# A linear attention and two expert MLPs: the W_out ring of eight swept forth and back, layer 2's conversion spread, g split half a step ahead

## The chip, the core and the metric

The kernel runs on one core of a Trainium2 chip. The metric is the device time of one execution in microseconds (us). TensorE (PE) multiplies, VectorE (DVE) and ScalarE (ACT) do the element-wise work, and SyncE (SP) issues nearly all DMAs, in the order in which they stand in its queue; GpSimd (POOL) does next to nothing.

## The reference

A linear attention with decay over 4 batches, 8 heads, 768 positions and head size 64 gives x of 3072 tokens by 512 features. Two MLPs follow it, each 512 to 2048 to 512:

```python
for t in range(S):
    state = gamma * state + einsum('bhd,bhe->bhde', k[:, :, t], v[:, :, t])
    y[:, :, t] = scale * einsum('bhd,bhde->bhe', q[:, :, t], state)
x = y as (3072, 512)
h = x @ w_in;   g = h * sigmoid(1.702 * h);                     x = g @ w_out      # layer 1
h = x @ w_in2;  g = max(h, 0) + alpha * min(h, 0);              x = g @ w_out2     # layer 2
```

The weights of the MLPs come as float64 and the output is float32.

## The kernel before, in words

**Precision.** Every operand of the MLPs is split into a high and a low half (fp32r); a product is hi·hi + hi·lo + lo·hi, three matmuls of 128x512. A weight slice (`in` or `out`, 16 of each per layer) comes as float64 words in a buffer `ld`; `conv_words`, `conv_f32`, `conv_hi` and `conv_lo` make the two halves on ACT and DVE, and for layer 2 `store` writes them to HBM at once (`wc` for W_in, `wo` for W_out). For W_in, `conv_sums` and `conv_split` add four sums of quarters per two slices (`shi`, `slo`, also stored into `wc`).

**Stages.** The first 250 us do the attention and the first two blocks of 512 tokens of layer 1. Then come five *pairs* of blocks, `PAIRS`: two of layer 1 and three of layer 2. A pair has 16 *half-steps*, numbered h = 0 to 79 over all pairs (`idx, q = divmod(h // 2, NQ)`): the even one is `quad_1`, 24 matmuls into PSUM tiles pa, px, pb, pd (L549), the odd one `quad_2`, 18 matmuls into pa, pb, pd. Seven products per two slices of W_in replace eight. Behind each product ACT or DVE adds (`u`, `u3`, `gw`, L571 to L604) and applies the activation, so that four tiles g come out of two half-steps. From half-step 9 on (`QLAG`), two *y-steps* follow each half-step: a y-step multiplies one tile g (128 features of the 2048, 512 tokens) with its slice of W_out, 12 matmuls into four tiles py (L473). 16 y-steps make a sweep, two sweeps (t = 0, 1) a pair. When the last half-step is done, 18 y-steps are left.

**g_split (L438, L439).** Before a y-step, ACT casts g to `gh` and DVE subtracts to get `gl`. `y_split` calls it for both y-steps of a half-step.

**Slots.** All these tiles but the W_in ring lie in 82 equal slots of 2 KB per partition. `take` pops the slot that has been free longest, `give` appends it. A tile that takes a slot must wait for the last reader of the tile before it: for `shi`, `slo`, `whi`, `wlo`, `wb` and `y` that is a DMA that stores them.

**Loads.** A pair's W_in comes as `g1` (1024 KB) and `g2` (768 KB) per two half-steps (`load_w`, L522 and L524), two ahead; each of the two buffers is free again when the product that reads it last is done. The slices of W_out come from HBM as `woh` and `wol` (256 KB each, `load_wo`, L543), one pair of tiles per y-step, four y-steps ahead (`WSTEPS`). The evacuated py goes out from `y` (L509) at the end of a sweep.

**Order.** A scheduler of the framework puts the instructions on the engines' queues; it follows priorities and its own idea of when each operand is ready. `W2_AT` is a table that says at which half-step each of the 32 conversions of layer 2 (m = 0 to 31) enters; m = 10 to 27 enter at half-steps 16 to 27.

Of the kernel before, what the change touches and what calls it, by code (L numbers as in the profile page):

```python
# [8 lines left out]
F32 = mybir.dt.float32  # L9
F32R = mybir.dt.float32r  # L10
# [13 lines left out]
NF = DFF // P  # L24
# [5 lines left out]
LEAD = 5  # L30
LAG = 1
QLAG = 9
WSTEPS = 4
WARM = 17
CS = 4
HP = 300
# [8 lines left out]
PAIRS = ((1, 1), (1, 2), (2, 0), (2, 1), (2, 2))  # L45
NQ = NF // 2
X_OF = ("b11", "t2", "t3", "t1", "b21", "t4", "b22")
ATT1 = 36
W2_AT = [7 + m // 2 for m in range(10)] + [16 + 2 * (m - 10) // 3 for m in range(10, 28)] + [34 + m - 28 for m in range(28, 32)]


@with_exitstack
def tile_linear_attention_two_mlps(ctx: ExitStack, tc, qk, kv, w1, w2, consts, alpha, out):
# [9 lines left out]
    nc = tc.nc  # L63
# [26 lines left out]
    wo = {  # L90
        (l, f): dram.tile([2, P, 512], F32, name=f"wo{l}_{f}", tag=f"wo{l}_{f}") for l in (1, 2) for f in range(NF)
    }
    stored = set()
# [4 lines left out]
    def take(name, shape=(P, 512), dtype=F32):  # L98
        i = free.popleft()
        t = spool.tile(list(shape), dtype, tag=f"s{i}", name=name)  # L100
        home[id(t)] = (i, t)
        return t

    def give(*ts):
        for t in ts:
            free.append(home.pop(id(t))[0])
# [329 lines left out]
    def g_split(g):  # L436
        gh, gl = take("gh", dtype=F32R), take("gl", dtype=F32R)
        nc.scalar.copy(out=gh, in_=g)  # L438
        nc.vector.tensor_tensor(out=gl, in0=g, in1=gh.bitcast(F32), op=ALU.subtract)  # L439
        give(g)  # L440
        return gh, gl
# [17 lines left out]
    def mlp_y(layer, j, ft, begin, end, carry, w):  # L459
        if begin:  # L460
            for e in range(NP):
                py[e] = ps_y.tile([P, BT], F32, tag=f"y{e}", name=f"py{e}")
        gh, gl = g_of.pop((layer, j, ft))
        wh, wl = w
        cols = lambda w, e: w[:, e * P:(e + 1) * P]
        prods = [(e, cols(w, e), gh) for e in range(NP) for w in (wh, wl)]
        prods += [(e, cols(wh, e), gl) for e in range(NP)]
        if carry == "last" or (end and carry == "first"):
            prods.sort(key=lambda p: p[0])
        seen = [0] * NP  # L470
        for e, w, g in prods:
            seen[e] += 1
            nc.tensor.matmul(  # L473
                out=py[e], lhsT=w, rhs=g, start=(begin and seen[e] == 1), stop=(end and seen[e] == 3)
            )
            if not end or seen[e] < 3:
                continue
            with tc.high_priority(HP):
                mlp_out(layer, j, e, carry)
        give(gh, gl)  # L480

    def mlp_out(layer, j, e, carry):
        y = take("y")
        if carry == "in":
            old = loaded["part", e // 2].rearrange("p (a b) -> p a b", a=2)[:, e % 2, :]
            nc.vector.tensor_tensor(out=y, in0=py[e], in1=old, op=ALU.add)
            if e % 2:
                done()
        elif carry == "last" and e == NP - 1:
            m = BT // 2  # L490
            nc.scalar.copy(out=y[:, :m], in_=py[e][:, :m])
            nc.vector.tensor_copy(out=y[:, m:], in_=py[e][:, m:])
            rows = slice(e * P, (e + 1) * P)
            nc.scalar.dma_start(out=out[rows, j * BT:j * BT + m], in_=y[:, :m])
            nc.sync.dma_start(out=out[rows, j * BT + m:(j + 1) * BT], in_=y[:, m:])
            return
        elif e % 2:
            nc.vector.tensor_copy(out=y, in_=py[e])
        else:
            nc.scalar.copy(out=y, in_=py[e])  # L500
        if carry == "out":
            dst = part[e // 2, :, e % 2, :]
        elif layer == 1:
            dst = xsd[2 + j // 2][e % 2, :, e // 2, j % 2, :]
            if e == NP - 1 and j % 2:
                stored.add(("x", 2 + j // 2))
        else:
            dst = out[e * P:(e + 1) * P, j * BT:(j + 1) * BT]
        (nc.scalar if carry == "last" and e % 2 else nc.sync).dma_start(out=dst, in_=y)  # L509
        give(y)  # L510
# [4 lines left out]
    def load_w(n):  # L515
        if n >= NQ * len(PAIRS):
            return
        layer, i = PAIRS[n // NQ][0], n % NQ
        need = [("in", layer, 2 * i), ("in", layer, 2 * i + 1), ("sums", layer, i)]
        assert all(k in stored for k in need), (n, need)  # L520
        g1 = xpool.tile([P, 4, 512], F32R, tag=f"xhi{(n + 1) % 2}", name="g1")
        nc.sync.dma_start(out=g1.bitcast(F32), in_=wc[layer, i][0:4].rearrange("g p c -> p g c"))  # L522
        g2 = xpool.tile([P, 4, 512], F32R, tag=f"xlo{(n + 1) % 2}", name="g2")
        nc.sync.dma_start(out=g2[:, 0:3].bitcast(F32), in_=wc[layer, i][4:7].rearrange("g p c -> p g c"))  # L524
        two = lambda t, u, n: tuple(t[:, m, 256 * n:256 * n + 256] for m in (u, u + 1))
        ring[n] = (
            two(g1, 0, 0), two(g1, 2, 1), two(g2, 0, 0), two(g1, 2, 0),
            two(g1, 0, 1), (g2[:, 2, 0:256], g2[:, 2, 256:512]), two(g2, 0, 1),
        )

    ysteps = [
        (idx, t, f) for idx in range(len(PAIRS)) for t in range(2) for f in range(NF)
    ]
    wring = {}

    def load_wo(n):
        if n >= len(ysteps):
            return
        layer, f = PAIRS[ysteps[n][0]][0], ysteps[n][2]
        assert ("out", layer, f) in stored  # L540
        wring[n] = take("woh", dtype=F32R), take("wol", dtype=F32R)
        for t, src in zip(wring[n], (0, 1)):
            nc.sync.dma_start(out=t.bitcast(F32), in_=wo[layer, f][src])  # L543

    def product(idx, q, n, ps, fresh):
        wh, wl = ring[idx * NQ + q][n]
# [63 lines left out]
    def y_split(n):  # L610
        idx, t, f = ysteps[n]
        with tc.high_priority(HG):
            g_of["y", t, f] = g_split(g_of.pop((idx, t, f)))

    def y_step(n):
        idx, t, f = ysteps[n]
        layer, pr = PAIRS[idx]
        carry = "last" if n == len(ysteps) - 1 else "first" if idx == len(PAIRS) - 1 else None
        g_of[layer, 2 * pr + t, f] = g_of.pop(("y", t, f))
        w = wring.pop(n)  # L620
        mlp_y(layer, 2 * pr + t, f, f == 0, f == NF - 1, carry, w)
        give(*w)
        load_wo(n + WSTEPS)


    per = BT // C
# [7 lines left out]
    def job(slot, fn, *args, load=()):  # L634
        jobs.setdefault(int(slot), []).append((fn, args, load))
# [8 lines left out]
    def convert(key, slot):  # L644
        job(slot, conv_words, key, load=(key,))
        job(slot + 1, conv_f32, key)
        job(slot + 2, conv_hi, key)
        job(slot + 2, conv_lo, key)
        if key[0] == "in" and key[2] % 2:
            i = key[2] // 2  # L650
            s = slot + 3 if key[1] == 2 else ATT1 + 1 + 4 * i if i < 4 else base + 2 * i - 6
            job(s, conv_sums, key[1], i)
            job(s + 1, conv_split, key[1], i)
# [11 lines left out]
    for ft in range(NF):  # L665
        pair = [("in", ft - ft % 2), ("in", ft - ft % 2 + 1), ("out", ft - ft % 2), ("out", ft - ft % 2 + 1)]
        for n, kind in enumerate(("in", "out")):
            m = 2 * ft + n
            lead = 2 * LEAD
            convert((kind, 1, ft), m - 2 * per + CS if ft < LEAD else lead + 1 + 1.1 * (m - lead))  # L670
            kind, f = pair[2 * (ft % 2) + n]
            convert((kind, 2, f), base + W2_AT[m])
            job(12 + m if ft < LEAD else ATT1 + 0.7 * (m - 10), store, (("in", "out")[n], 1, ft))
# [32 lines left out]
    def run(slot):  # L706
        todo = [(rank.index(fn) if fn in rank else len(rank), i) for i, (fn, _, _) in enumerate(jobs.get(slot, ()))]
        for _, i in sorted(todo):
            fn, args, _ = jobs[slot][i]
            fn(*args)  # L710
# [24 lines left out]
    def drop():  # L735
        for _ in range(len(waiting)):
            key = waiting.popleft()
            if key in stored:
                give(w_hi.pop(key), w_lo.pop(key))
            else:  # L740
                waiting.append(key)
# [17 lines left out]
        if s == NF + LEAD:  # L759
            load_w(0)  # L760
    load_w(1)
    for n in range(WSTEPS):
        load_wo(n)
    for s, step in queue:
        finish_step(s, step)
    drop()
    done_y = 0
    for h in range(2 * NQ * len(PAIRS)):
        idx, q = divmod(h // 2, NQ)
        if h >= QLAG:  # L770
            for n in range(2):
                y_split(done_y + n)
        (quad_2 if h % 2 else quad_1)(idx, q)
        run(base + h)
        drop()
        if h >= QLAG:
            for n in range(2):
                y_step(done_y)
                done_y += 1
    for n in range(done_y, len(ysteps)):  # L780
        y_split(n)
        y_step(n)


# [51 lines left out]
```

## Time and profile before

| | us |
|---|---|
| median of 3 runs | 1124.21 |
| lowest, highest | 1120.92, 1129.53 |
| the profiled execution | 1124.57 |
| its span | 1122.8 |

The profiled execution spends 1.8 us outside its span. PE is busy 1092.6 us (97%), DVE 678.2 (60%), ACT 548.2 (49%). TensorE's clock was granted in full but for one stretch in the middle. A DMA share of 1.0 means that all 16 DMA engines were busy all the time.

### The profile page before, as it was taken

Reading aid. Unit: us, or ns where it says so; the run is one execution under the profiler, and the core shown is the slowest. Engines: PE = TensorE matmul, PEld = TensorE weight load, DVE = VectorE, ACT = ScalarE, POOL = GpSimd, SP = SyncE. Lnnn points to the kernel's source line nnn. Section 1 sums busy time; section 2 is a strip of 40 time slices with the busy share of each in tenths; the row PEclk is TensorE's granted clock in tenths of the full one; section 3 lists DMA queues with packets and bytes.
Section 4 is the critical chain, followed back from the end, with each engine's and each line's share of the span. In section 5 each row is a group of like instructions: output and inputs, shape, how many; then the busy total and the mean of one; then the engine's idle time right before and its main releaser. Section 6 shows DMA issues by size and latency. Waiting matters only on the chain.

```text
span 1122.8 us, 15612 instructions
## 1 busy us (share of the span) xinstructions
PE 1092.6 (97%) x5633; PEld 897.8 (80%) x5633; DVE 678.2 (60%) x1162; ACT 548.2 (49%) x1081; POOL 0.2 (0%) x4
## 2 busy tenths in 40 slices
PE   8899999999999999997999999999999999999998
PEld 6688787888888877875887888888888888888887
DVE  6899855365688785756666555764454764353530
ACT  7787745254575554544545444453343553343520
POOL 0000000000000000000000000000000000000000
PEclk9999999999999999998999999999999999999999
DMA  8899979278999979979979879568647377556731
GB/s 294 270 302 289 302 271 311 84 266 308 334 305 372 361 264 376 353 252 384 346 258 348 313 272 313 160 232 282 188 158 255 130 238 251 183 206 220 218 129 37
DMA packets 146700, 292.88 MB, mean 261 GB/s; under 512 B 13120, under 2 KB 23744, under 8 KB 146624
## 3 DMA queue, kind: packets, MB, share of 16 engines
q1 hardware_dynamic: 146192, 291.43, 75.7%
q8 instruction: 44, 0.72, 0.3%
q10 hardware_dynamic: 432, 0.47, 0.1%
q14 instruction: 32, 0.26, 0.1%
HBM read 227.88 MB, written 63.96 MB: 260 GB/s over the span
## 4 chain that ended last, share of the span: by engine, by line
PE 81%; DMA 11%; ACT 3%; DVE 3%; SPq 2%; issue 1%; DVEq 0%; ACTq 0%
PE py L473 42%; PE pb L549 9%; PE pd L549 8%; PE pa L549 8%; PE ph L450 5%; PE px L549 4%; DMA ld<-w 4%; DMA wc<-shi 2%; PE px L314 1%; PE sc L281 1%; PE px L304 1%; DMA wc<-wb 1%; DMA wc<-slo 1%; DMA g<-wc 1%; DMA wol<-wo 1%
## 5 line engine op out<-in xcount | busy, mean ns | idle before, releaser
L473 PE MATMUL py<-gh,woh 128*128 128x512 f32 x640 | 243.4, 391 | 11.8 <-ACT gh L438 10.9
L473 PE MATMUL py<-gh,wol 128*128 128x512 f32 x640 | 243.0, 390 | 1.0 <-DMA wol<-wo 1.0
L473 PE MATMUL py<-gl,woh 128*128 128x512 f32 x640 | 172.0, 389 | 0.0
L439 DVE TENSOR_TENSOR gl<-gw,gh 128x512 fp32r<-128x512 f32 x160 | 108.1, 688 | 95.1 <-ACT gh L438 76.2
L438 ACT CAST gh<-gw 128x512 fp32r<-128x512 f32 x160 | 97.6, 617 | 135.1 <-PE py L473 91.5
L473 PEld LDWEIGHTS py<-gh,woh 128*128 128x128 f32 x640 | 120.6, 189 | 38.1 <-ACT gh L438 11.8
L473 PEld LDWEIGHTS py<-gh,wol 128*128 128x128 f32 x640 | 120.7, 189 | 26.4 <-DMA wol<-wo 1.4
L473 PEld LDWEIGHTS py<-gl,woh 128*128 128x128 f32 x640 | 120.1, 188 | 25.0
L431 DVE SCALAR_TENSOR_TENSOR gw<-t,nalpha,gw 128x512 f32<-128x512 f32 x96 | 72.0, 750 | 78.2 <-ACT gw L430 77.9
L429 ACT ACTIVATE t<-gw 128x512 f32<-128x512 f32 x72 | 45.2, 628 | 100.8 <-DVE gw L580 81.3
L549 PE MATMUL pb<-xohi,g 128*128 128x512 f32 x320 | 86.3, 390 | 2.8 <-DMA g<-wc 2.8
L549 PE MATMUL pa<-xohi,g 128*128 128x512 f32 x320 | 87.6, 393 | 0.2 <-DMA g<-wc 0.2
L549 PE MATMUL pd<-xohi,g 128*128 128x512 f32 x320 | 85.8, 389 | 0.0
L549 PEld LDWEIGHTS pb<-xohi,g 128*128 128x128 f32 x320 | 59.8, 188 | 16.4 <-DVE cvt L166 3.6
L549 PEld LDWEIGHTS pd<-xohi,g 128*128 128x128 f32 x320 | 60.0, 188 | 12.9 <-ACT xohi L388 0.4
L549 PEld LDWEIGHTS pa<-xohi,g 128*128 128x128 f32 x320 | 59.3, 188 | 13.6 <-DMA g<-wc 0.6
L274 ACT ACTIVATE v<-ld,cst 128x64 f32<-128x64 f32 x168 | 44.4, 336 | 33.1 <-DMA ld<-kv 32.8
L156 ACT ACTIVATE cvt<-ld 128x512 f32<-128x512 f32 x64 | 43.0, 671 | 32.2 <-DMA ld<-w 20.5
L574 DVE TENSOR_TENSOR u<-px,u 128x512 f32<-128x512 f32 x40 | 27.6, 689 | 45.8 <-PE px L549 41.0
L473 PE MATMUL py<-gh,whi 128*128 128x512 f32 x128 | 51.9, 406 | 2.1 <-ACT gh L438 2.1
L450 PE MATMUL ph<-xhi,whi 128*128 128x512 f32 x128 | 51.4, 401 | 1.6 <-ACT xhi L360 1.5
L473 PE MATMUL py<-gh,wlo 128*128 128x512 f32 x128 | 50.3, 393 | 0.0
(92 smaller groups left out, 1679.6 us busy)
## 6 DMA issues: line engine op xcount, KB each, us to landing
g<-wc SPq DMA_DIRECT2D x40, 1024.0 KB, 7.0
woh<-wo SPq DMA_DIRECT2D x160, 256.0 KB, 5.2
wol<-wo SPq DMA_DIRECT2D x160, 256.0 KB, 5.3
ld<-w SPq DMA_DIRECT2D x64, 512.0 KB, 5.4
g<-wc SPq DMA_DIRECT2D x40, 768.0 KB, 6.7
ld<-qk SPq DMA_DIRECT2D x21, 512.0 KB, 5.1
ld<-kv SPq DMA_DIRECT2D x21, 512.0 KB, 4.8
ld<-xsd SPq DMA_DIRECT2D x20, 512.0 KB, 6.4
```

Of the source, the lines that this page charges most:

```text
L156: nc.scalar.activation(out=t, in_=w1, func=AF.Abs, scale=2.0**-112)
L274: nc.scalar.activation(out=v[:, h, :], in_=vt[:, h * D:(h + 1) * D], func=AF.Copy, scale=decay_v[:, h:h + 1])
L281: nc.tensor.matmul(out=ps[s][:, p, :], lhsT=kt[r, p * C:(p + 1) * C], rhs=qt[r, p * C:(p + 1) * C], start=True, stop=True,)
L304: nc.tensor.matmul(out=px[:, p, :], lhsT=state[:, p, :], rhs=qt[:, p * C:(p + 1) * C], start=(p == 0), stop=False, skip_group_check=True,)
L429: nc.scalar.activation(out=t, in_=src, func=AF.Relu, scale=-1.0)
L431: nc.vector.scalar_tensor_tensor(out=g, in0=t, scalar=nalpha[:, ft:ft + 1], in1=g, op0=ALU.mult, op1=ALU.add)
L438: nc.scalar.copy(out=gh, in_=g)
L439: nc.vector.tensor_tensor(out=gl, in0=g, in1=gh.bitcast(F32), op=ALU.subtract)
L450: nc.tensor.matmul(out=ph, lhsT=w[:, k * P:(k + 1) * P], rhs=x[:, k, :], start=(n == 0), stop=(n == len(prods) - 1),)
L473: nc.tensor.matmul(out=py[e], lhsT=w, rhs=g, start=(begin and seen[e] == 1), stop=(end and seen[e] == 3))
L549: nc.tensor.matmul(out=ps, lhsT=w[:, k * P:(k + 1) * P], rhs=xo[idx, n, k][part_], start=(fresh and m == 0), stop=(m == len(prods) - 1), s ...
L574: nc.vector.tensor_tensor(out=u, in0=px, in1=u, op=ALU.add)
```

## The change

Three edits.

- `WSTEPS` goes from 4 to 8, and the second sweep of each pair runs through the slices backwards. The ring is now keyed by layer and slice: a slice that is used again within the next 16 y-steps stays, so that the eight slices of a turning point are loaded once for both sweeps. `load_wo` fills the ring up to eight slices as soon as places are free. 96 slices are loaded in all, where 160 were.
- In `W2_AT`, m = 10 to 21 enter at half-steps 16 to 27, one each, and m = 22 to 31 at half-steps 32 to 39, in the third pair.
- `y_split` for the y-steps of half-step h is emitted behind quad h - 1, ahead of the y-steps of h - 1; it was emitted ahead of quad h.

```diff
-WSTEPS = 4
+WSTEPS = 8
...
-W2_AT = [7 + m // 2 for m in range(10)] + [16 + 2 * (m - 10) // 3 for m in range(10, 28)] + [34 + m - 28 for m in range(28, 32)]
+W2_AT = [7 + m // 2 for m in range(10)] + [16 + m - 10 for m in range(10, 22)] + [32 + 4 * (m - 22) // 5 for m in range(22, 32)]
...
     ysteps = [
-        (idx, t, f) for idx in range(len(PAIRS)) for t in range(2) for f in range(NF)
+        (idx, t, f if t == 0 else NF - 1 - f) for idx in range(len(PAIRS)) for t in range(2) for f in range(NF)
     ]
+    wkey = [(PAIRS[idx][0], f) for idx, _, f in ysteps]
     wring = {}
 
     def load_wo(n):
-        if n >= len(ysteps):
-            return
-        layer, f = PAIRS[ysteps[n][0]][0], ysteps[n][2]
-        assert ("out", layer, f) in stored
-        wring[n] = take("woh", dtype=F32R), take("wol", dtype=F32R)
-        for t, src in zip(wring[n], (0, 1)):
-            nc.sync.dma_start(out=t.bitcast(F32), in_=wo[layer, f][src])
+        for key in wkey[n:n + 2 * WSTEPS]:
+            if key in wring:
+                continue
+            if len(wring) == WSTEPS or ("out",) + key not in stored:
+                return
+            wring[key] = take("woh", dtype=F32R), take("wol", dtype=F32R)
+            for t, src in zip(wring[key], (0, 1)):
+                nc.sync.dma_start(out=t.bitcast(F32), in_=wo[key][src])
...
-        w = wring.pop(n)
-        mlp_y(layer, 2 * pr + t, f, f == 0, f == NF - 1, carry, w)
-        give(*w)
-        load_wo(n + WSTEPS)
+        mlp_y(layer, 2 * pr + t, f, n % NF == 0, n % NF == NF - 1, carry, wring[wkey[n]])
+        if wkey[n] not in wkey[n + 1:n + 2 * WSTEPS]:
+            give(*wring.pop(wkey[n]))
+        load_wo(n + 1)
...
-    for n in range(WSTEPS):
-        load_wo(n)
+    load_wo(0)
...
-    done_y = 0
+    split = 0
     for h in range(2 * NQ * len(PAIRS)):
         idx, q = divmod(h // 2, NQ)
-        if h >= QLAG:
-            for n in range(2):
-                y_split(done_y + n)
         (quad_2 if h % 2 else quad_1)(idx, q)
         run(base + h)
         drop()
+        if h >= QLAG - 1:
+            for n in range(split, split + 2):
+                y_split(n)
+            split += 2
         if h >= QLAG:
-            for n in range(2):
-                y_step(done_y)
-                done_y += 1
-    for n in range(done_y, len(ysteps)):
-        y_split(n)
+            for n in range(split - 4, split - 2):
+                y_step(n)
+    for n in range(split - 2, len(ysteps)):
+        if n + 2 < len(ysteps):
+            y_split(n + 2)
         y_step(n)
```

**Place 1, PE, half-steps 24 to 26 (in the second pair).** Matmuls of a quad (L549 before, L551 now) and of a y-step (py). Before:

```order
L473 MATMUL py_4559<-gl,woh 128x512
L473 MATMUL py_4560<-gl,woh 128x512
L549 MATMUL pd<-xohi,g_4923 128x512 x4
L549 MATMUL pd<-xolo,g_4923 128x512 x2
L549 MATMUL pa<-xohi,g_5131 128x512 x4
L549 MATMUL pa<-xolo,g_5131 128x512 x2
L549 MATMUL px<-xohi,g_5131 128x512 x4
L549 MATMUL px<-xolo,g_5131 128x512 x2
L549 MATMUL pa<-xohi,g_5131 128x512 x4
L549 MATMUL pa<-xolo,g_5131 128x512 x2
L473 MATMUL py_5379<-gh,woh 128x512
```

Now:

```order
L473 MATMUL py_4541<-gl,woh 128x512
L473 MATMUL py_4542<-gl,woh 128x512
L551 MATMUL pa<-xohi,g_4871 128x512 x4
L551 MATMUL pa<-xolo,g_4871 128x512 x2
L551 MATMUL pb<-xohi,g_4873 128x512 x4
L551 MATMUL pb<-xolo,g_4873 128x512 x2
L551 MATMUL pd<-xohi,g_4873 128x512 x4
L551 MATMUL pd<-xolo,g_4873 128x512 x2
L473 MATMUL py_5249<-gh,woh 128x512
```

Before, products of three quads stand between the y-steps of half-steps 24 and 25; now it is the one quad of 25. From half-step 17 to the end PE now reads quad, two y-steps, quad, two y-steps; before, it did so from half-step 36 on.

**Place 2, SP, the end of the second pair's first sweep (half-steps 24 and 25).** L509 stores the y of the sweep, and waits for its last y-step. Before:

```order
L524 DMA g_5133<-wc_5_94 128x3x512
L509 DMA xsd_87<-y 128x512 x4
L207 DMA wo_8_129<-whi 128x512
L207 DMA wo_8_129<-wlo 128x512
L126 DMA ld<-w 128x1024 x2
L543 DMA woh<-wo_0_105 128x512
L543 DMA wol<-wo_0_105 128x512
L543 DMA woh<-wo_1_106 128x512
L543 DMA wol<-wo_1_106 128x512
L247 DMA wc_4_101<-shi 128x512
L248 DMA wc_4_101<-slo 128x512
```

Now:

```order
L509 DMA xsd_87<-y 128x512 x4
L522 DMA g_5223<-wc_6_95 128x4x512
L524 DMA g_5225<-wc_6_95 128x3x512
L545 DMA woh<-wo_8_113 128x512
L545 DMA wol<-wo_8_113 128x512
L545 DMA wol<-wo_9_114 128x512
L207 DMA wo_8_129<-wlo 128x512
L545 DMA wol<-wo_10_115 128x512
L545 DMA woh<-wo_11_116 128x512
L545 DMA wol<-wo_11_116 128x512
L247 DMA wc_4_101<-shi 128x512
```

The stores of the sums (wc_4) still stand behind the y, but the W_in load for half-step 28 and later tiles stand between, and no slot of these sums goes to a `gh` or `gl` now.

**Place 3, ACT, half-steps 11 and 12 (in the first pair).** L438 casts gh, L571 (now L573) evacuates pa of quad 12. Before:

```order
L438 CAST gh_4075<-gw_3645 128x512
L438 CAST gh_4071<-gw_3637 128x512
L571 COPY u_3977<-pa_3973 128x512
L438 CAST gh_4175<-gw_3875 128x512
L438 CAST gh_3969<-gw_3446 128x512
```

Now:

```order
L244 CAST shi_4129<-s12_4029 128x512
L156 ACTIVATE cvt_3945<-ld_3821 128x512
L157 ACTIVATE cvr_3946<-ld_3821 128x512
L185 CAST whi_4125<-cvt_3941 128x512
L438 CAST gh_3953<-gw_3462 128x512
L573 COPY u_3993<-pa_3989 128x512
```

gh_3969 and gh_3953 are the same thing, the gh of half-step 12's second y-step. Before, it has the slot of the first of the four sums stored in half-step 11, and the evacuation of pa stands ahead of it; now it has the slot of the last of the four, and the evacuation stands behind it.

## Rows read from the trace of the kernel before

**Rows 1.** The page: the span, and busy time and share of each engine.

```profile
span 1122.8 us, 15612 instructions
PE 1092.6 (97%) x5633; PEld 897.8 (80%) x5633; DVE 678.2 (60%) x1162; ACT 548.2 (49%) x1081; POOL 0.2 (0%) x4
```

**Rows 2.** Waits of PE: who ended them; us in total, times, longest us.

```profile
PE py L473 <- ACT gh L438: 13.0, 5, 10.6
PE pb L549 <- DMA g<-wc: 2.8, 2, 1.7
...
PE py L473 <- DMA wol<-wo: 1.0, 1, 1.0
```

**Rows 3.** Timeline of PE: start, duration; first y-step of half-steps 9, 37, 57.

```profile
329.71 0.39 PE L473 MATMUL py<-gh,woh 128*128 128x512 f32 x1
...
635.89 0.39 PE L473 MATMUL py<-gh,woh 128*128 128x512 f32 x1
...
839.89 0.39 PE L473 MATMUL py<-gh,woh 128*128 128x512 f32 x1
```

**Rows 4.** Windows: stretch, length, busy us per engine, clock, DMA share, GB/s.

```profile
325.00:350.00 25.00, 25.00 (x120) 20.62 (x115) 24.16 (x49) 16.39 (x29) 0.00 (x0) 1.00 0.93 332
350.00:375.00 25.00, 24.69 (x110) 20.09 (x109) 17.43 (x32) 13.62 (x26) 0.00 (x0) 1.00 1.02 354
...
500.00:525.00 25.00, 14.40 (x58) 11.49 (x57) 15.46 (x30) 12.10 (x22) 0.00 (x0) 0.80 1.03 369
525.00:550.00 25.00, 25.00 (x112) 20.71 (x111) 15.30 (x27) 9.33 (x17) 0.00 (x0) 1.00 1.04 384
575.00:600.00 25.00, 23.08 (x101) 18.44 (x100) 18.83 (x32) 14.80 (x27) 0.00 (x0) 1.00 0.69 220
600.00:625.00 25.00, 25.00 (x112) 20.68 (x111) 12.40 (x20) 9.54 (x16) 0.00 (x0) 1.00 1.00 357
625.00:650.00 25.00, 25.00 (x112) 20.70 (x111) 16.21 (x27) 11.68 (x21) 0.00 (x0) 1.00 0.85 314
650.00:675.00 25.00, 25.00 (x112) 20.71 (x111) 13.76 (x21) 11.84 (x22) 0.00 (x0) 1.00 0.72 246
```

**Rows 5.** Timeline, 497 to 515 us; in brackets the idle time before and who ended it.

```profile
497.72 1.81 SPq L509 DMA_DIRECT2D xsd<-y  x4
...
505.48 0.44 SPq L248 DMA_DIRECT2D wc<-slo  x1
...
512.82 1.25 ACT L438 CAST gh<-gw 128x512 fp32r<-128x512 f32 x2 [4.16 <-DMA wc<-slo]
...
513.49 0.80 PE L473 MATMUL py<-gh,woh 128*128 128x512 f32 x1 [10.60 <-ACT gh L438]
...
514.51 0.63 PE L473 MATMUL py<-gh,woh 128*128 128x512 f32 x1
...
514.94 0.63 PE L473 MATMUL py<-gh,wol 128*128 128x512 f32 x1
```

**Rows 6.** DMA issues by line: count, KB each, median us from issue to landing.

```profile
woh<-wo SPq DMA_DIRECT2D x160, 256.0 KB, 5.2
wol<-wo SPq DMA_DIRECT2D x160, 256.0 KB, 5.3
ld<-w SPq DMA_DIRECT2D x64, 512.0 KB, 5.4
...
wc<-slo SPq DMA_DIRECT2D x32, 256.0 KB, 6.1
```

**Rows 7.** Timeline of first y-steps (12, 14) and stores (11, 13) in the first pair.

```profile
356.50 1.07 SPq L248 DMA_DIRECT2D wc<-slo  x1
...
360.99 0.39 PE L473 MATMUL py<-gh,woh 128*128 128x512 f32 x1
...
364.86 0.50 PE L473 MATMUL py<-gh,woh 128*128 128x512 f32 x1 [0.31 <-ACT gh L438]
...
380.12 0.33 SPq L247 DMA_DIRECT2D wc<-shi  x1
...
382.69 0.62 PE L473 MATMUL py<-gh,woh 128*128 128x512 f32 x2
```

**Rows 8.** Lines L247 and L248, 330 to 395 us: from issue to landing.

```profile
DMA to landing us min/median/max: 8.6/9.6/10.4
...
DMA to landing us min/median/max: 6.3/9.2/10.3
```

## The prediction

> **What bounds the kernel now.** I read the page's first part, then PE's waits, then PE's timeline for its rhythm, then windows for the place of the loss. PE is busy 97% of the span [rows 1], and all that its waits name is late operands: 13.0 us for gh, of which one wait is 10.6, and 2.8 us for W_in [rows 2]. The rhythm shows how much is to be had. From the first y-step of half-step 37 to that of 57, 204.0 us pass, 10.20 per half-step [rows 3], and the windows there show PE busy throughout [rows 4]. From half-step 9 to 37, 306.18 us pass [rows 3], where 28 half-steps at 10.20 are 285.6. So 20.6 us are lost between 330 and 636 us, and nothing that the change touches is lost behind that. Before half-step 9 it touches only four early loads of W_out and two g_splits. A version with no loss would take 1124.57 - 20.6 = 1104.0 us. This is the floor.
>
> Where the 20.6 us lie: the largest piece is one event. SP stands at the y store until the sweep's last y-step has run, 497.72 us, and then sends a burst; the store of `slo` goes out at 505.48, ACT's gh needs that store's slot and waits for its landing, and PE stands 10.60 us, until 513.49 [rows 5]. The granted clock of that window is 0.80 on average [rows 4]: behind the idle stretch the matmuls start 0.43 us apart, 514.51 and 514.94 [rows 5], where 0.227 is usual; eight of them cost 1.6 us more. The rest are W_in and W_out that come late while the DMA engines are full: shares of 1.02 to 1.04 at 354 to 384 GB/s between 350 and 550 us [rows 4].
>
> **The change, part by part.** All sums are against the profiled execution, 1124.57 us, which is 0.36 above the median.
>
> *The ring.* 160 - 96 = 64 slices fewer are loaded, two tiles of 256 KB each [rows 6]: 64 x 2 x 262 KB = 33.6 MB, some 90 us of full DMA engines at 369 GB/s [rows 4]. Nothing is loaded for y-steps in half-steps 13 to 16, 21 to 24 and 29 to 32, and a slice comes eight y-steps (41 us) ahead, not four. The four more slices loaded up front go out before half-step 0, ahead of the second W_in on SP; 8 issues of some 0.4 us and 2.1 MB cost W_in perhaps 6 us there, which has a whole quarter of cover; I take nothing.
>
> *The conversions.* From half-step 16 to 28 there are 12 in place of 18, so that the conversions and the ring together leave DMA free there. Ten instead of four now lie at half-steps 32 to 39, that is about 575 to 660 us.
>
> *g_split.* gh and gl of a half-step are emitted 24 matmuls (5.4 us) earlier. ACT and DVE do the same casts and subtractions. Place 1 of the change shows that the scheduler no longer needs to fill with later quads: from half-step 17 on, every quad's evacuation has a full half-step of y-steps as cover.
>
> *What I take for the middle (half-steps 16 to 35):* of the loss there everything comes back. The sums stored behind the y (place 2) give their slots to W_out tiles with eight y-steps' notice, no longer to gh; W_in is far ahead. Bounds: 0 and, for a stray late load, the 2.8 us that W_in cost before [rows 2]. I take 0.
>
> *What it costs: slots.* The ring holds 8 more slots, and gh and gl live longer. Following `take` and `give` through the code, the fewest free slots fall from 12 to 4 in half-steps 9 to 12, and from 16 to 6 in half-steps 36 to 38. A slot comes round after 5 to 12 takes, where it was 13 to 25; more tiles take a slot whose store is still under way. Two places count.
>
> First pair. In half-steps 9 to 12 the work for DMA is the same as before (the conversions there do not move, the ring loads two slices per half-step), and DMA is full [rows 4]. Stores take 9 to 10 us to land [rows 8]. The gh of half-step 12's second y-step now has the slot of the last `slo` (place 3). That store went out at 356.50 [rows 7] and lands up to 10.3 us later [rows 8]: 366.8. With the cast (0.6 us by the two casts in 1.25 us [rows 5]) PE can go on at 367.4. The y-step before starts at 360.99 [rows 7] and has 12 matmuls of 0.227 us (10.20 / 45 per half-step, a half-step being 21 + 24), so it would go on at 363.7; before, it did at 364.86 [rows 7]. I take 3.8 us lost here, where 1.2 were lost. The gh of half-step 14 has the slot of the `shi` stored at 380.12 [rows 7]; at 9.6 us [rows 8] that lands at 389.7, with the cast 390.3. The second y-step would start at 382.69 - 1.2 + 12 x 0.227 + 8 x 0.227 (eight matmuls stand between) = 386.0, with 3.8 carried over 389.8. I take 1 us more with the subtraction behind. Sum 5 us; bounds 0 (stores land in the usual 6.1 us [rows 6]: 362.6, too early to matter) and 12 (DVE is busy 24.16 of 25 us at 325 to 350 [rows 4], so what it stands there comes back late as a whole: twice the 4.16 of a slot wait [rows 5] and the 3.8).
>
> Third pair. 575 to 675 us carry (220 + 357 + 314 + 246) / 4 = 284 GB/s [rows 4]. Six more conversions bring 6 x 0.52 MB of words [rows 6] and about 4 MB of stores, 7.1 MB in 82 us or 87 GB/s. The ring saves nothing there, because it turns over to layer 2's slices. 371 GB/s is just under the 384 seen [rows 4]. In half-step 38 gh and gl take slots of sums stored in it. I take 2 us, bounds 0 and 12.2 (the event of rows 5 again: 10.6 and 1.6 of slow clock).
>
> The sum: 1124.57 - 20.6 + 0 + 5 + 2 = **1111 us**, 13 below the median.
>
> On the third pair the Trainium skill speaks against the change: Perfetto Trace Analysis, Identifying Performance Opportunities, says that a gap that repeats on the engine that should be saturated can mean that there isn't enough SBUF for the next tile. The rows of before show no such repeating gap, and here the change takes eight slots; by that sentence the cost would recur, as in rival C.
>
> **The rivals.**
>
> *A. Stores land in time, nearly all comes back.* If they land in 6.1 us [rows 6] in place of 9 to 10, the first pair loses nothing, the third neither: 1104 to 1107. For it: 64 slices fewer. Against: in half-steps 9 to 12 not one byte less is moved, and the engines are full [rows 4]. Perfetto Trace Analysis (Trainium skill), Engine Utilization, gives a single active core about 435 GB/s as the ceiling of its DMA engines; with that, the first pair's DMA would have room. The trace disagrees: at a share of 1.02 to 1.04 it shows 354 to 384 GB/s [rows 4]. Chance 0.2.
>
> *B. The stall moves to the third pair.* The y store holds SP back at half-steps 32 and 40 as it did at 24; the sums of half-step 38 go out late, ACT's gh waits for them, and with it the activations behind it on ACT. Price 12.2 instead of 2: 1121; with the first pair at its bound 1126. For it: DMA at its limit with 6 free slots. Against: the W_out tiles no longer press. Chance 0.25.
>
> *C. Slower: SP itself stands.* In half-steps 9 to 12 and 37, 38 and 40, `woh` and `wol` take slots whose store went out just ahead on SP, so SP stands until it has landed, up to 10.4 us [rows 8] per half-step of 10.2, and the W_in load behind it is late. W_in has a quarter (20.4 us) of cover, and that decides: four such stands are 41 us, less 20.4 leaves 20.6; three in the third pair 31, less 20.4 leaves 10.6. 1104 + 31 = 1135, plus what the slots cost: up to 1142. Against: part of each stand overlaps the time in which SP has nothing to send anyway. Chance 0.07.
>
> *D. The edits do nothing,* since the stall is the y store's and this stays ahead on SP (place 2): 1124. The order speaks against it, since no gh hangs on what follows. It lies within B's range, and its chance (0.03 of B's 0.25) is with B.
>
> **How the numbers follow.** Forecast 0.48, 1107 to 1116; A 0.2, 1104 to 1107; B 0.25, 1116 to 1126; C 0.07. The three executions of before spread from 1120.92 to 1129.53, so that about 1% is what a measurement can tell: 1113.0 and 1135.5 are the limits. Of the forecast some six tenths lie under 1113: 0.29 with A's 0.2 is 0.49 for faster, 0.46 for the same, 0.05 for slower. The range leaves out C and the upper half of B: 1104 to 1122.
>
> **What would show it.** Right: no wait of PE over 3 us between 400 and 560 us; 10.20 us per half-step from 17 on; `woh` and `wol` 96 times each; DMA shares well under 1 at half-steps 13 to 24; PE waits for gh near half-step 12 whose gh waited for `slo`. Wrong: an 8 to 12 us wait near half-steps 38 to 41 (B), W_in as the releaser of PE at half-steps 12 to 15 (C), or no wait at all (A). If the y-steps' rhythm before half-step 9 moved, my floor would be off.

## The result

| | median, us | lowest to highest | runs |
|---|---|---|---|
| before, same chip | 1123.78 | 1120.92 to 1131.34 | 16 |
| changed | 1114.84 | 1111.80 to 1121.65 | 16 |

The ratio is 0.9915, 95% interval 0.9897 to 0.9934: 0.85% faster. The profiled execution took 1114.78 us, its span 1113.0. The forecast was 1111 us, with 1104 to 1122 as the range. The time lies in the forecast's own case (1107 to 1116), but two of its terms were off in opposite directions and made up for each other in part. The gain it put down to the ring and the table together; the experiments show that either alone is enough for it.

### The profile page after: what moved, and what is told of

It is laid out like the page before. It is cut to its first block, busy times and chain, and to the rows that moved or that the text cites. A ratio compares the mean times of both kernels' runs of the same rounds, so it can differ in the third digit from the quotient of the medians.

```text
span 1113.0 us, 15358 instructions
## 1 busy us (share of the span) xinstructions
PE 1092.1 (98%) x5633; PEld 897.9 (81%) x5633; DVE 683.2 (61%) x1162; ACT 549.4 (49%) x1081; POOL 0.2 (0%) x4
## 4 chain that ended last, share of the span: by engine, by line
PE 81%; DMA 11%; DVE 3%; ACT 3%; issue 1%; SPq 0%; DVEq 0%; ACTq 0%
PE py L473 43%; PE pa L551 8%; PE pd L551 8%; PE pb L551 8%; DMA ld<-w 5%; PE ph L450 5%; PE px L551 4%; DMA ld<-kv 3%; DMA wc<-shi 2%; PE px L314 1%; PE sc L281 1%; PE px L304 1%; ACT v L274 1%; DMA wc<-wlo 1%; PE idle L729 1%
## 5 line engine op out<-in xcount | busy, mean ns | idle before, releaser
L473 PE MATMUL py<-gh,woh 128*128 128x512 f32 x640 | 250.0, 391 | 0.0
L473 PE MATMUL py<-gh,wol 128*128 128x512 f32 x640 | 249.7, 390 | 0.0
L473 PEld LDWEIGHTS py<-gh,wol 128*128 128x128 f32 x640 | 120.7, 189 | 25.1
L438 ACT CAST gh<-gw 128x512 fp32r<-128x512 f32 x160 | 96.8, 617 | 53.0 <-PE py L473 21.6
L551 PE MATMUL pa<-xohi,g 128*128 128x512 f32 x320 | 87.2, 393 | 0.0
L551 PE MATMUL pb<-xohi,g 128*128 128x512 f32 x320 | 85.9, 389 | 0.0
L551 PE MATMUL pd<-xohi,g 128*128 128x512 f32 x320 | 85.7, 389 | 0.0
L551 PEld LDWEIGHTS pb<-xohi,g 128*128 128x128 f32 x320 | 60.1, 188 | 12.5
L551 PEld LDWEIGHTS pd<-xohi,g 128*128 128x128 f32 x320 | 60.1, 188 | 12.5
L551 PEld LDWEIGHTS pa<-xohi,g 128*128 128x128 f32 x320 | 59.4, 188 | 13.0 <-issue 0.2
L573 ACT COPY u<-pa 128x512 f32<-128x512 f32 x40 | 23.4, 586 | 73.6 <-PE pa L551 67.7
```

What stands on the lines that cost most here:

```text
L473: nc.tensor.matmul(out=py[e], lhsT=w, rhs=g, start=(begin and seen[e] == 1), stop=(end and seen[e] == 3))
L551: nc.tensor.matmul(out=ps, lhsT=w[:, k * P:(k + 1) * P], rhs=xo[idx, n, k][part_], start=(fresh and m == 0), stop=(m == len(prods) - 1), s ...
L573: nc.scalar.copy(out=u, in_=pa)
```

## The profile after

The page: span, then busy time, share and instructions of each engine [rows 1].

```profile
span 1113.0 us, 15358 instructions
PE 1092.1 (98%) x5633; PEld 897.9 (81%) x5633; DVE 683.2 (61%) x1162; ACT 549.4 (49%) x1081; POOL 0.2 (0%) x4
DMA packets 128267, 259.31 MB, mean 233 GB/s; under 512 B 11072, under 2 KB 21696, under 8 KB 128192
```

PE has the same work, and DMA moves 33.6 MB less. The timeline of PE has the first y-step of half-steps 9, 37 and 57 [rows 3] at:

```profile
330.12 0.39 PE L473 MATMUL py<-gh,woh 128*128 128x512 f32 x1
...
626.11 0.39 PE L473 MATMUL py<-gh,woh 128*128 128x512 f32 x1
...
830.11 0.39 PE L473 MATMUL py<-gh,woh 128*128 128x512 f32 x1
```

From 37 to 57 it is 204.0 us as before. From 9 to 37 it is 295.99, so that 295.99 - 285.6 = 10.4 us are lost, where 20.6 were. I use this one number, the *loss*, for every kernel below. The waits of PE say what it consists of [rows 2] (us in total, times, longest):

```profile
PE py L473 <- DVE gl L439: 7.0, 2, 5.4
PE py L473 <- ACT gh L438: 3.7, 3, 2.2
```

Both waits for gl lie in the first pair, at 347.99 us (half-step 10) and 370.90 us (half-step 12); those for gh lie before 254 us, where the loss is not counted. The windows [rows 4] show where the loss isn't:

```profile
325.00:350.00 25.00, 23.34 (x113) 18.77 (x114) 24.83 (x51) 16.93 (x31) 0.00 (x0) 1.00 0.93 334
350.00:375.00 25.00, 19.62 (x79) 15.68 (x78) 17.38 (x32) 11.46 (x20) 0.00 (x0) 0.88 0.98 342
...
500.00:525.00 25.00, 25.00 (x112) 20.70 (x111) 17.15 (x30) 12.40 (x21) 0.00 (x0) 1.00 0.96 327
525.00:550.00 25.00, 25.00 (x112) 20.70 (x111) 12.31 (x20) 8.91 (x15) 0.00 (x0) 1.00 0.69 253
575.00:600.00 25.00, 25.00 (x112) 20.72 (x111) 19.57 (x32) 14.70 (x26) 0.00 (x0) 1.00 0.78 268
600.00:625.00 25.00, 25.00 (x112) 20.68 (x112) 18.98 (x36) 14.17 (x26) 0.00 (x0) 1.00 0.95 327
625.00:650.00 25.00, 25.00 (x112) 20.72 (x111) 20.01 (x34) 16.11 (x30) 0.00 (x0) 1.00 0.97 333
650.00:675.00 25.00, 25.00 (x112) 20.72 (x111) 15.42 (x26) 11.12 (x21) 0.00 (x0) 1.00 0.88 311
```

Only the second window has PE much below 25 us, with a granted clock of 0.88. From 375 us on PE never stands. Of the event of [rows 5] at 500 to 515 us nothing is left, and the third pair, where ten conversions now lie, carries (268 + 327 + 333 + 311) / 4 = 310 GB/s and stalls nobody.

The stall at 370.90 can be followed through the engines' timelines. In brackets is the idle time before and who ended it:

```profile
357.51 0.53 SPq L247 DMA_DIRECT2D wc<-shi  x1
...
360.01 0.32 SPq L247 DMA_DIRECT2D wc<-shi  x1
360.68 0.51 SPq L248 DMA_DIRECT2D wc<-slo  x1
...
367.83 0.67 ACT L156 ACTIVATE cvt<-ld 128x512 f32<-128x512 f32 x1 [6.67 <-DMA wc<-shi]
...
368.52 0.43 DVE L163 TENSOR_SCALAR cvt<-cvt 128x512 f32<-128x512 f32 x1 [5.77 <-ACT cvt L156]
...
370.16 0.68 DVE L439 TENSOR_TENSOR gl<-gw,gh 128x512 fp32r<-128x512 f32 x1
...
370.90 2.07 PE L473 MATMUL py<-gl,woh 128*128 128x512 f32 x4 [5.38 <-DVE gl L439]
372.77 0.63 PE L473 MATMUL py<-gh,woh 128*128 128x512 f32 x1
373.20 0.63 PE L473 MATMUL py<-gh,wol 128*128 128x512 f32 x1
```

Read from the bottom: PE waits for gl, gl stands on DVE behind a conversion, the conversion waits for ACT, and ACT stands at the conversion's scratch tile `cvt`, whose slot held a `shi` until its store had landed. The wait is of the first y-step of half-step 12. The chain of waits has the same pieces, with that landing as the longest:

```profile
351.12 6.32 DMA ld<-w
...
357.51 10.29 DMA wc<-shi
...
367.83 0.67 ACT cvt L156
...
370.24 0.61 DVE gl L439
...
370.90 5.23 PE py L473 x12
```

Behind the wait the matmuls start 0.43 us apart (372.77, 373.20), the lower of TensorE's two levels, 1.2 GHz, where 0.227 is usual at 2.4. From 370.90 to the 13th at 375.97 it is 5.07 us in place of 12 x 0.227 = 2.72: 2.35 us more. So the loss is 1.66 + 5.38 + 2.35 = 9.4 of the 10.4; the rest is short gaps around these.

## The experiments

Of each kernel there are the ratio to before on the same chip, and from its profiled execution the loss and the start of half-step 9's first y-step, up to which the kernels differ by 7 us through waits in the first stage. Each loss and start is of one execution; for the table alone it is the slowest of four (1110.61 us). The two tell nearly all: before has 329.71 + 20.58, changed 330.12 + 10.39, and both take 774.3 us beyond that (1124.57 and 1114.78).

| ring | table | split | | median, us | ratio, 95% | start | loss |
|---|---|---|---|---|---|---|---|
| - | - | yes | split alone | 1127.22 | 1.0012, 0.9988 to 1.0036 | 333.35 | 21.4 |
| yes | - | - | ring alone | 1111.79 | 0.9878, 0.9837 to 0.9919 | 332.01 | 6.0 |
| - | yes | - | table alone | 1107.32 | 0.9848, 0.9808 to 0.9888 | 332.71 | 3.4 |
| - | yes | yes | without the ring | 1111.65 | 0.9884, 0.9843 to 0.9925 | 332.82 | 5.7 |
| yes | yes | - | without the split | 1111.64 | 0.9864, 0.9832 to 0.9897 | 329.76 | 7.2 |
| yes | yes | yes | changed | 1114.84 | 0.9915, 0.9897 to 0.9934 | 330.12 | 10.4 |

### One edit at a time

Ring alone: the changed kernel with the table and the place of g_split as before.

> The ring alone: eight slices forth and back; the table of conversions and the place of g_split as before. Theory (the ring ends the loss, because 33.6 MB fewer press on the DMA engines between half-steps 13 and 32): 1112 to 1117 us, no wait of PE over 3 us between 400 and 560 us, and the wait near half-step 12 stays. Rival (the wait of gh on a sum's store comes from the order of the work, and the bytes don't matter): 1120 to 1125 us, with a wait of 8 to 11 us near 500 us.

1111.79 us, at the lower edge of the theory. Nothing is lost from half-step 17 on, and 6.0 us before. The theory holds for this kernel.

Table alone: before with one line changed.

```diff
-W2_AT = [7 + m // 2 for m in range(10)] + [16 + 2 * (m - 10) // 3 for m in range(10, 28)] + [34 + m - 28 for m in range(28, 32)]
+W2_AT = [7 + m // 2 for m in range(10)] + [16 + m - 10 for m in range(10, 22)] + [32 + 4 * (m - 22) // 5 for m in range(22, 32)]
```

> The table of conversions alone: 12 in place of 18 in half-steps 16 to 28, ten in place of four behind 32; ring of four and g_split as before. Theory (bytes in the middle): a conversion moves about 1.2 MB, so 6 fewer take out 7 MB of the ring's 33.6, a fifth: 1118 to 1123 us, with W_in or gh still late for some us between 400 and 560 us. Rival (the table alone empties the middle): 1112 to 1116 us. Second rival (it only moves the stall into the third pair): 1122 to 1128 us, with a wait of 8 to 12 us behind 600 us.

1107.32 us, loss 3.4. My theory is wrong here, and the first rival is right in kind, its range even too high: without one byte less for W_out the table alone does more than the whole change, whose interval (0.9897 to 0.9934) lies wholly above this one's (0.9808 to 0.9888), if narrowly. The largest wait of PE after half-step 9 is 1.1 us, although the DMA engines are as full as before:

```profile
425.00:450.00 25.00, 25.00 (x112) 20.71 (x111) 14.97 (x28) 10.19 (x18) 0.00 (x0) 1.00 1.03 388
...
500.00:525.00 25.00, 25.00 (x111) 20.44 (x110) 13.04 (x21) 11.33 (x20) 0.00 (x0) 1.00 1.02 382
```

Split alone: before with the new loop around `y_split`.

> g_split half a step ahead alone; ring and table as before. Theory (bytes in the middle): nothing is moved less, and gh and gl hold their slots longer: 1121 to 1127 us, the wait of about 10 us near 500 us stays. Rival (the regular order is what ends the loss, since an operand that is due earlier has 5 us more of cover): 1113 to 1118 us.

1127.22 us, loss 21.4: no gain, as the theory had it. But its wait of about 10 us did not stay; it became two, 2.86 us for woh at 507.88 and 2.04 for wol at 510.63.

Without the ring: table and split.

> The change without its ring: table and g_split as changed, ring of four as before, all slices in the same order. Theory (the ring's bytes): 1118 to 1124 us; 160 loads of woh and wol, DMA shares over 1 between 400 and 550 us, and PE waits there of 5 us or more. The wait near half-step 12, where the ring's eight slots are missing, falls to 2 us or less. Rival (table and g_split carry the gain): 1108 to 1115 us.

1111.65 us, loss 5.7. The theory is wrong again: the shares are over 1 (1.04 at 382 and 398 GB/s between 425 and 475 us), but the longest wait of PE there is 0.96 us. At half-step 12 nobody waits any more; at 13 PE waits 0.87 us for woh.

Without the split: ring and table.

> Ring and table without the early g_split, the fourth of the combinations. Theory (the ring's eight slots cost in the first pair and give nothing that the table hasn't given): between the table alone and the changed kernel, 1110 to 1114 us, of which the ring's price is 3 to 6 us and lies in half-steps 10 to 13. Rival (the loss of the changed kernel in the first pair is the early g_split's, which holds gh and gl longer): 1106 to 1109 us, as the table alone.

1111.64 us, loss 7.2, all of it before half-step 17. So beside this table the ring would cost 7.2 - 3.4 = 3.8 us and the split 3.2 more. These sizes hang on one profile each. The medians stand in the same order (1107.32, 1111.64, 1114.84), but the intervals of neighbours overlap; only that the two together cost something is clear of noise.

### Bytes or crowding

The table takes six conversions out of the middle, and thins them from 1.5 to 1 in a half-step. The first experiment was meant to put the bytes back, without conversions:

```diff
+    extra = {h: dram.tile([P, 1024], I32, name=f"extra{h}", tag=f"extra{h}") for h in range(16, 29)}
...
         run(base + h)
+        if h in extra:
+            nc.sync.dma_start(out=extra[h], in_=src_of(("in", 1, h - 16)))
```

> The table alone (as in the run before of that edit, 1107 us), with 13 transfers added that nothing waits for: 0.52 MB each from DRAM to DRAM, one in every half-step from 16 to 28 on SP, 6.8 MB, about what the six conversions moved out of the middle bring. PE's order is the same. Theory (the table helps by the bytes that it takes from the DMA engines there): the loss comes back, 1115 to 1123 us, with PE waits for W_in, W_out or gh of 5 us or more between 400 and 560 us. Rival (the table helps by the number of conversions on ACT, DVE and in the slots, and by the regular order that this allows): 1106 to 1110 us.

It does not do that. Nothing holds these transfers back, and they stand on SP's queue far ahead of the half-steps at which the code names them. All 13 go out between 25.1 and 204.4 us, in the first stage:

```profile
L777 SPq DMA_DIRECT2D extra<-w x13: 488/587/917, 25.1 to 204.4; - x13
```

So this run says nothing of bytes in the middle, and tests neither the theory nor the rival. Its median is 1112.98 us (1108.75 to 1115.18); the profiled execution, the fastest, has a loss of 2.5.

The second puts the crowd back, without the number:

```diff
-... + [16 + m - 10 for m in range(10, 22)] + ...
+... + [16 + 2 * (m - 10) // 3 for m in range(10, 22)] + ...
```

> The table alone, with its 12 middle conversions put 1.5 to a half-step from 16 on, as before, so that they are through at half-step 23 in place of 27. Number and bytes in the middle as in the table alone, the crowd until half-step 24 as before. Theory (the crowd counts, not the number: what is late at half-step 24 is what piled up until then): 1117 to 1124 us, the wait near 500 us is back. Rival (the number counts; there is no backlog left from half-step 16): 1106 to 1112 us.

1120.51 us, ratio 0.9952, 0.9933 to 0.9971; loss 14.3. Twelve conversions in 8 half-steps lose 11 us more than twelve in 12. The stall is back near the same place, with the slow clock behind it (matmuls 0.43 us apart at 513.18 and 513.61):

```profile
503.13 0.43 DVE L233 TENSOR_TENSOR s<-cvt 128x256 f32<-128x256 f32 x1 [1.70 <-DMA xsd<-y]
...
504.73 0.45 SPq L543 DMA_DIRECT2D woh<-wo  x1
...
507.01 0.69 DVE L245 TENSOR_TENSOR slo<-s,shi 128x512 fp32r<-128x512 f32 x1 [1.26 <-ACT shi L244]
...
507.74 0.69 DVE L597 TENSOR_TENSOR gw<-pb,u 128x512 f32<-128x512 f32 x1
...
508.49 1.65 PE L549 MATMUL pb<-xohi,g 128*128 128x512 f32 x3 [3.47 <-DVE gw L597]
...
511.31 1.22 PE L473 MATMUL py<-gh,woh 128*128 128x512 f32 x2 [1.17 <-DMA woh<-wo]
```

Two things are late. One is `gw`: it stands on DVE behind the sums, whose first waited for the landing of a `y` that is stored, and which wait for ACT in between. This is the same kind of chain as in the first pair of the changed kernel. The other is a slice of W_out: SP issued it at 504.73 only, because it had stood 14.2 us at the y store ahead of it.

So the crowded table brings the loss back. But it brings back more than the work on ACT and DVE. Twelve conversions in 8 half-steps also move their bytes in 8. And the order on the queues, which is fixed before the kernel runs, becomes that of before again up to half-step 24. In three kernels, before, split alone and this one, the four stores of the sums stand on SP 4 to 10 us behind the y store near 500 us, and products of later quads stand between the y-steps on PE until half-step 28 or 35. In all others no such store goes out in the 12 us behind that y store, and PE's order is regular from half-step 21 on at the latest. Those three are also the only kernels in which PE waits more than 0.3 us anywhere behind half-step 20. Which of these counts, the bytes in a half-step, the slots, the work on ACT and DVE or the order, no run separates.

### What is left in the first pair

There the first ten conversions lie two to a half-step, in all kernels so far. Two ways to free it. One lets gh, gl, gw, t, u, u3 and the conversions' scratch pass over slots that held a stored tile:

```diff
-        i = free.popleft()
+        i = next((s for s in free if last.get(s) not in STORED), free[0]) if late and name in FRESH else free[0]
+        free.remove(i)
+        last[i] = name
```

> The changed kernel, whose gh, gl, gw, t, u, u3 and conversions' scratch take the oldest free slot that held no stored tile, where there is one. Theory (the 10 us that the changed kernel still loses are waits for the landing of a store in a reused slot): 1106 to 1110 us, no wait of PE over 1.5 us between 340 and 380 us. Rival (DMA is simply full there, and W_out or W_in come late in place of gl): 1112 to 1117 us, with PE waiting for woh, wol or g.

1112.38 us, ratio 0.9869, 0.9834 to 0.9904; loss 7.5. That is the rival's time, but not its releasers: the wait of half-step 10 is gone, that of half-step 12 is still 5.05 us, for gl, which still got the slot of a `shi` (DVE stood 4.89 us for it). Perhaps too few slots are free for every tile to find another; this is not shown.

The other spreads the conversions, one to a half-step from 7 on, in the changed kernel:

```diff
-W2_AT = [7 + m // 2 for m in range(10)] + [16 + m - 10 for m in range(10, 22)] + ...
+W2_AT = [7 + m for m in range(10)] + [17 + m - 10 for m in range(10, 22)] + ...
```

> The changed kernel with the first ten conversions put one to a half-step (7 to 16, the next twelve 17 to 28) in place of two. Theory (crowding sets what is late, in the first pair as in the second: the 10 us lost in half-steps 10 to 13 hang on two conversions in one half-step): 1104 to 1108 us, no wait of PE over 1.5 us between 340 and 380 us. Rival (the ring's eight slots and the early g_split take the slots, whatever the conversions do): 1111 to 1116 us, with the wait for gl near 370 us.

1103.68 us, ratio 0.9818, 0.9794 to 0.9843; loss 0.0. The same even table in the kernel before, with nothing else changed:

> The kernel before with nothing but the table changed, and that wholly even: one conversion in each of half-steps 7 to 28, ten behind 32. Ring of four, g_split as before. Theory (the conversions' crowding is all that was lost): 1102 to 1106 us, PE's rhythm 10.20 us per half-step from 9 to 37 with 0 to 2 us lost. Rival (without the ring the four-slice W_out comes late while the DMA engines are full): 1107 to 1112 us, PE waiting for woh or wol.

1104.06 us, ratio 0.9838, 0.9810 to 0.9866; loss 0.0. One line does all that the three edits were to do, and neither kernel can be told from the other. The first y-steps of half-steps 9 and 37 in this last kernel, and its fullest windows:

```profile
329.85 0.39 PE L473 MATMUL py<-gh,woh 128*128 128x512 f32 x1
...
615.45 0.39 PE L473 MATMUL py<-gh,woh 128*128 128x512 f32 x1
```

```profile
425.00:450.00 25.00, 25.00 (x112) 20.67 (x112) 13.56 (x24) 11.58 (x20) 0.00 (x0) 1.00 1.04 396
...
500.00:525.00 25.00, 25.00 (x112) 20.68 (x111) 12.38 (x20) 8.91 (x15) 0.00 (x0) 1.00 1.04 397
```

615.45 - 329.85 = 285.6 is 28 half-steps at 10.20 exactly, with a share of 1.04 and nobody late. Its chain of waits, 500 to 520 us, is PE alone, quad and y-steps in turn, no quad run ahead:

```profile
504.09 5.44 PE py L473 x24
509.53 1.36 PE pa L549 x6
510.89 1.36 PE pb L549 x6
512.25 1.36 PE pd L549 x6
513.61 5.44 PE py L473 x24
```

The even table with the ring, without the split:

> The same even table with the ring of eight, without the early g_split. Theory (with an even table the ring has nothing left to give or to cost): within 3 us of the even table alone. Rival (its eight slots still cost in the first pair): 3 to 6 us more than that.

1108.84 us, ratio 0.9864, 0.9842 to 0.9886: 4.8 more than the even table alone, so the rival's number. Between the profiled executions it is 5.7, and only 2.3 of that is loss, mostly a wait of 1.96 us for gh at 346.28. The other 3.4 is a later start (333.28), which the ring does not explain: the other kernels with it start at 328.75 to 332.01. The two intervals overlap, and two of the six executions of the even table alone took as long (1108.66 and 1109.99). Undecided, then: with the split on top the loss is 0.0 again.

At last the bytes once more, on the even table, 20 transfers that were meant for half-steps 9 to 28:

> The even table alone (1104 us), with 20 transfers added that nothing waits for: 0.52 MB each from DRAM to DRAM, one in every half-step from 9 to 28 on SP, 10.5 MB. Theory (bytes alone cost little while the conversions are even, since the reads come ahead and the stores have cover): 1103 to 1107 us, at most 3 us lost from half-step 9 to 37. Rival (bytes do cost; the table with 13 such transfers came out at 1113 us where the table without them had 1107): 1108 to 1116 us, with PE waiting for woh, wol, g or gh.

1109.96 us, ratio 0.9862, 0.9836 to 0.9889: the rival's number. But these transfers, too, went out in the first stage, the last of them 116 us ahead of half-step 9:

```profile
L777 SPq DMA_DIRECT2D extra<-w x20: 488/587/1203, 24.6 to 219.8; - x20
```

That the loss behind half-step 9 is 0.0 says nothing of added bytes, then: from 325 to 575 us this kernel moves 335 GB/s, the one without the transfers 333. What the run does show is in the first stage. Half-step 9's first y-step starts at 335.71, 5.9 us later than with the even table alone. One piece of this hangs on the transfers:

```profile
154.03 0.53 SPq L127 DMA_DIRECT2D ld<-kv  x1
...
156.76 3.06 SPq L777 DMA_DIRECT2D extra<-w  x3
...
161.85 0.35 ACT L275 ACTIVATE v<-ld,cst 128x64 f32<-128x64 f32 x1 [3.71 <-DMA ld<-kv]
...
164.18 1.13 PE L305 MATMUL px<-ld,state 128*128 128x128 f32 x8 [2.63 <-DVE a L292]
```

A load of k and v goes out among six of them and lands after 7.80 us, where the same load takes 3.50 with the even table alone; ACT, DVE and at last PE wait for it, PE 2.63 us. The rest of the 5.9 is no more than what kernels without such transfers differ by at this place (328.75 to 333.35); where that comes from was not tried. So whether bytes in the middle cost anything with even conversions stays open.

## Why the prediction was right and wrong

**The floor: right.** 1104.0 us was worked out as the time without any loss; two kernels with none have 1104.06 and 1103.68. A third, with the 20 transfers, has 1109.96, by its later start: that the early stage would stay where it was holds only within 7 us.

**The middle, 0: right in size, half right in reason.** I put the return of the loss down to ring and table together, the ring's bytes first. Ring alone ends the loss from half-step 17 on, but the table alone, with the DMA engines at 1.03, leaves no wait over 1.1 us there either. So fewer bytes for W_out were not needed for it. In the changed kernel they were there: the DMA shares came out as 0.80 to 0.93 between 375 and 475 us. What the table changes is how many conversions stand in one half-step: each moves bytes, takes slots, stores tiles and queues work on ACT and DVE between gh and gl. Which of these counts most is not separated here, since a crowded table always changed all of them, and the order on PE and SP as well. Nor was it tried whether fewer bytes alone help a crowded table; the ring takes 128 tiles out of the slots' turn together with its bytes. And neither kernel with added transfers had them in the middle.

**The first pair, 5: the step that failed, by size.** I took a wait of gh for the store of `slo` "at 356.50" and 3.8 us at half-step 12; with the 1 at half-step 14 that made 5. It is 10.4. The half-step and the kind of wait, for a store's landing in a reused slot, were right; the operand was not, gl of the first y-step and not gh of the second. Three things made it larger. The stores are not where they were: SP issues them from 357.51 to 360.68, behind W_out loads in its queue that had themselves waited up to 1.4 us for slots whose `slo` had not landed, and they land at 367.80 to 370.03, not 366.8. The tile that stood first was not gh but a conversion's `cvt`; ACT stood 6.67 us at it, DVE 5.77 behind it, and gl, the second half of the operand, was behind both. And the slow clock, which I priced at 1.6 us in [rows 5], I left out of this term: 2.35 us. The wait at half-step 10 (1.66) I hadn't seen at all; at half-step 14 PE did not stand.

**The third pair, 2: too much.** It lost 0. My sum of 371 GB/s came out as 310, and PE did not stand once. The page of the Trainium skill that spoke against the change (Perfetto Trace Analysis, Identifying Performance Opportunities) takes a gap that repeats as a possible sign of too little SBUF. There is no gap in the third pair. In the first pair there are two, and the longer one did hang on a reused slot. In the shorter one gl stood behind conversions on a DVE that had not been idle since 339.73; that this wait is gone where tiles pass over slots of stored ones speaks for a slot there too, but does not show it.

**The rivals.** A's time (1104 to 1107) was open, but by another door than faster landings: the stores of half-step 11 still take 9 to 10 us. B's stall in the third pair didn't come. Of C one piece was there, SP late by up to 4 us at its stores, without W_in ever being late. D is out: the edits do something, and one of them, the table, is enough.

## What to carry to other kernels

Before moving fewer bytes, spread the side work: conversions at one per step in place of two, a table of 32 numbers, took the whole loss of 20.6 us at full DMA engines, and more buffering on top gave nothing. Full DMA engines were not a loss in themselves here. In the longest stalls, 10.6 us before and 5.38 after, a store had to land before a tile that PE needed could be made, so look at who stands in the queues of SP, ACT and DVE between that landing and the operand. Try the edits of a change one by one: here two of three together made the one that paid slower (0.9915 against 0.9848). And look up in the trace when an added instruction runs: the code named half-steps 9 to 28, and the transfers ran before 220 us.

## What the runs showed of the hardware

A DMA share of 1.04 at 396 GB/s for 25 us went by without one late operand, where 1.03 at 369 GB/s stood beside a stall of 10.6 us in the kernel before [rows 4, 5]; the share doesn't tell the two apart. In the changed kernel the wait of 5.38 us was followed by matmuls 0.43 us apart until 375.33 us, 2.35 us on top of its length; the one of 1.66 us was followed by none. A load of k and v that went out among six added transfers of 0.52 MB landed after 7.80 us, where it took 3.50 without them.
